# R's low channels as row tiles beside K, and the mix as two vector operations, in a convolution and channel-mix kernel

## Chip, cores, metric

The kernel runs on one core of one Trainium2 chip. The metric is the device time of one execution in microseconds (us), the median of several. The run-to-run spread of the kernel before is about 0.3%. Engines in what follows: PE is the tensor engine, PEld its weight loads, DVE the vector engine, ACT the scalar engine, POOL GpSimd, SP the engine that issues most of the stores and the transposing reads.

## The reference

x has 8 batches of 4160 tokens with 192 channels. A causal convolution over 7 tokens, with one softmaxed filter for each of 8 heads of 24 channels, gives y. Then comes a channel mix with 1024 hidden channels:

```python
x_prev = shift_by_one_token(y)
xk = mu_k * y + (1 - mu_k) * x_prev
xr = mu_r * y + (1 - mu_r) * x_prev
k = np.maximum(xk @ w_k, 0.0)            # 192 -> 1024
v = k * k @ w_v                          # 1024 -> 192
r = 1.0 / (1.0 + np.exp(-(xr @ w_r)))    # 192 -> 192
out = r * v
```

## The kernel before

Batches are worked in four pairs. The 192 channels are split in 128 high ones (rows 0 to 127 of a tile) and 64 low ones; the low channels of the pair's two batches share one tile, rows 0 to 63 and 64 to 127. A *step* is 512 tokens of both batches; it takes four *bundles* of two *slots*, each slot 128 hidden channels of K for 1024 columns. At each pair's end a *tail* step does the last 64 tokens.

The low part of K runs as two 64-row matmuls side by side (row tiles). R uses full-height matmuls for both parts; for its low part the weight rows that belong to the other batch are zero:

```python
def k_mm(n):                                   # one slot; cut
    for f in range(nf):
        for i in range(2):
            r = slice(0, P) if hi else slice(i * LO, (i + 1) * LO)
            nc.tensor.matmul(out=ps[:, i, f * L : (f + 1) * L],
                             lhsT=wk[r, 0 if hi else 1, fs], rhs=xk[r, i if hi else 2, :L], ...)

def r_mm(m):                                   # one tile of 128 tokens of one batch; cut
    hi, lo, wlo = xr[:, st, c : c + P], xr[:, 2, c : c + P], wr[:, 2 + st, :]
    nc.tensor.matmul(out=o, lhsT=hi, rhs=wr[:, 0, :], start=True, stop=False)
    nc.tensor.matmul(out=o, lhsT=lo, rhs=wlo, start=False, stop=True)
```

A mix is one vector operation on the difference of neighbouring tokens:

```python
nc.vector.scalar_tensor_tensor(out=o, in0=d[r0:r1, sl, :L], scalar=mu[r0:r1, i, part : part + 1],
                               in1=yT[r0:r1, sl, c0 : c0 + L], op0=ALU.mult, op1=ALU.add)
```

The convolution runs ahead of K on PE in *groups* of 112-token blocks, several *chunks* of heads a group. ACT copies each chunk out of PSUM; the group is written to DRAM and read back transposed by DMA (the first groups of the first pair are transposed on PE instead). The kernel uses 8 banks of PSUM, the memory that matmuls write to: K holds two tiles of two banks, V two of one bank, and convolution, transposes and R share two tiles of one bank (`psM`, `bufs=2`).

## Time and profile before

| | kernel before |
|---|---|
| time, median of 4 runs | 469.4 us |
| span of the profiled run | 467.2 us |
| PE / DVE / ACT busy | 95% / 84% / 80% |
| PE's share of the chain that ended last | 91% |

PE is the bound. The lines that carry this stand in the prediction. The chain is followed back from the last instruction; an engine with a large busy share that is missing from it costs nothing at present (of this chain ACT has 2% and DVE 1%). For the comparison later, here are the stretches from one tail step's K to the next: start to the first tail, three pairs (the third, left out, takes 109.24 us like the second), and the drain (columns: stretch, length, then busy time and count of PE, PEld, DVE, ACT, POOL, granted PE clock, DMA share, GB/s).

```profile
0.00:128.87 128.87, 117.58 (x972) 76.38 (x987) 101.84 (x168) 100.13 (x158) 28.57 (x43) 0.97 0.93 152
128.87:238.11 109.24, 107.05 (x942) 72.18 (x955) 95.52 (x149) 92.62 (x134) 9.84 (x12) 1.00 0.75 153
...
347.35:453.25 105.90, 103.72 (x925) 70.25 (x939) 92.60 (x144) 85.45 (x116) 2.85 (x4) 1.00 0.43 108
453.25:467.20 13.95, 9.80 (x124) 9.57 (x122) 4.90 (x9) 3.80 (x7) 0.00 (x0) 0.93 0.28 93
```

The last pair is 3.3 us shorter because half of the convolution is left to do: 16 matmuls instead of 32. The 16 that are missing have 480 columns; at about 0.2 us each, an estimate from the 0.18 us between starts at 432 columns, they make 3.2 us.

### The profile page before, as it was taken

The page shows a single profiled execution, that of the slowest core. Times are in us where ns is not written, and L with a number is a line of the kernel's source. Part 1 is how long each engine was busy: PE and PEld are TensorE (multiplying, and loading weights), DVE is VectorE, ACT ScalarE, POOL GpSimd, SP SyncE. Part 2 cuts the span into 40 slices and gives each one's busy share as a digit, 9 for nine tenths or more (in the row PEclk, how much of TensorE's full clock was granted, in tenths as well). Part 3 has the DMA queues.
Part 4 walks back from the last instruction along what each step waited for, and adds up shares of the span by engine and source line. Part 5 has one row for each costly group of instructions (what it writes and reads, how often), then busy time and mean ns, then how long its engine had stood idle before and what let it go on. Part 6 is the DMA issues. An engine that isn't in the chain of part 4 may idle for free.

```text
span 467.2 us, 9868 instructions
## 1 busy us (share of the span) xinstructions
PE 445.2 (95%) x3892; PEld 300.6 (64%) x3954; DVE 390.4 (84%) x616; ACT 374.6 (80%) x549; POOL 51.1 (11%) x71
## 2 busy tenths in 40 slices
PE   7788999999999999999999999999999999999996
PEld 3454766666776666666676666666676666666676
DVE  2778988797998879889798989978898987999873
ACT  2489888988879797888879788888978888777771
POOL 5812211000010041000002041000002000000000
PEclk9799999999999999999999999999999999999999
DMA  7996699972459599945367679937157753511222
GB/s 89 160 174 106 162 197 156 233 200 68 127 142 183 148 139 229 181 129 139 93 173 119 165 133 214 229 100 187 52 152 138 173 135 100 153 65 56 69 69 94
DMA packets 138942, 65.79 MB, mean 141 GB/s; under 512 B 89936, under 2 KB 138464, under 8 KB 138896
## 3 DMA queue, kind: packets, MB, share of 16 engines
q1 hardware_dynamic: 98000, 49.26, 41.0%
q0 software_dynamic: 40896, 15.90, 30.0%
q8 instruction: 31, 0.51, 0.4%
q14 instruction: 15, 0.12, 0.1%
HBM read 31.59 MB, written 37.52 MB: 148 GB/s over the span
## 4 chain that ended last, share of the span: by engine, by line
PE 91%; ACT 2%; issue 2%; DMA 2%; DVE 1%; DVEq 0%; ACTq 0%
PE ps_k L343 38%; PE ps_v L433 37%; PE ps_c L199 5%; PE ps_r L416 5%; PE ps_r L415 5%; ACT k_sb L372 1%; DMA w_scr<-w_row 1%; PE ps_k L360 1%; DMA toe<-w_scr 1%; ACT y L219 1%; DMA w_raw<-in_weight_dram 1%; PE ps_t L257 1%; DVE yT L268 0%; ACT y L222 0%; DVE k L391 0%
## 5 line engine op out<-in xcount | busy, mean ns | idle before, releaser
L372 ACT ACTIVATE k_sb<-ps_k 128x1024 bf16<-128x1024 f32 x260 | 260.2, 1026 | 35.8 <-PE ps_k L343 31.8
L343 PE MATMUL ps_k<-xk,wk 64*128 64x512 bf16 (+2 forms) x994 | 206.0, 376 | 9.5 <-ACT k_sb L372 0.9
L433 PE MATMUL ps_v<-wv,k 128*128 128x192 bf16 x2048 | 210.8, 246 | 0.0
L433 PEld LDWEIGHTS <-k 128*128 128x128 bf16 x2048 | 175.4, 98 | 30.6 <-issue 1.4
L391 DVE TENSOR_TENSOR k<-k_sb 128x1024 bf16<-128x1024 bf16 x256 | 174.8, 684 | 16.7 <-ACT k_sb L372 16.0
L343 PEld LDWEIGHTS <-wk 64*128 64x128 bf16 (+1 forms) x1056 | 56.2, 96 | 109.2 <-issue 107.9
L446 DVE TENSOR_TENSOR o_sb<-ps_v,r_sb 128x384 f32<-128x384 f32 x132 | 72.2, 547 | 39.6 <-PE ps_v L433 34.7
L423 ACT ACTIVATE r_sb<-ps_r 128x384 bf16<-128x384 f32 x132 | 64.3, 487 | 38.1 <-PE ps_r L416 37.3
L301 DVE SCALAR_TENSOR_TENSOR xr<-d,mu,yT 128x1024 bf16<-128x1024 bf16 (+1 forms) x66 | 65.1, 988 | 0.1
L301 DVE SCALAR_TENSOR_TENSOR xk<-d,mu,yT 128x1024 bf16<-128x1024 bf16 (+1 forms) x66 | 64.4, 977 | 0.2
L415 PE MATMUL ps_r<-wr,xr 128*128 128x192 bf16 x256 | 62.8, 246 | 0.0
L416 PE MATMUL ps_r<-wr,xr 128*128 128x192 bf16 x256 | 62.8, 246 | 0.0
L219 ACT CAST y<-ps_c 112x480 bf16<-112x480 f32 (+4 forms) x100 | 47.9, 483 | 10.4 <-PE ps_c L199 10.2
L199 PE MATMUL ps_c<-xb,toe 128*112 128x480 bf16 (+5 forms) x152 | 46.2, 332 | 5.3 <-DMA toe<-w_scr 2.9
L109 POOL DMA_DIRECT2D xb<-in_x_dram x38 | 34.9, 928 | 26.8 <-PE ps_c L199 15.9
L281 DVE TENSOR_TENSOR d<-yT 128x1536 bf16<-128x1536 bf16 (+2 forms) x37 | 31.8, 859 | 0.4 <-DMA yT<-y_dram 0.2
L108 POOL DMA_DIRECT2D xb<-in_x_dram x8 | 4.3, 538 | 215.7 <-PE ps_k L343 206.3
L199 PEld LDWEIGHTS <-toe 128*112 128x112 bf16 x152 | 19.2, 134 | 12.1 <-DMA toe<-w_scr 3.4
L222 ACT CAST y<-ps_c 112x480 bf16<-112x480 f32 (+8 forms) x53 | 25.2, 482 | 0.2 <-DVE yT L227 0.2
L415 PEld LDWEIGHTS <-xr 128*128 128x128 bf16 x256 | 25.0, 98 | 0.0
L416 PEld LDWEIGHTS <-xr 128*128 128x128 bf16 x256 | 25.0, 98 | 0.0
L103 POOL DMA_DIRECT2D xb<-in_x_dram x8 | 4.6, 581 | 62.4 <-PE ps_r L416 61.0
(46 smaller groups left out, 67.8 us busy)
## 6 DMA issues: line engine op xcount, KB each, us to landing
out_dram<-o_sb SPq DMA_DIRECT2D x128, 192.0 KB, 2.3
y_dram<-y SPq DMA_DIRECT2D x7, 840.0 KB, 5.0
xb<-in_x_dram POOLq DMA_DIRECT2D x12, 432.0 KB, 12.0
y_dram<-y SPq DMA_DIRECT2D x6, 756.0 KB, 4.6
xb<-in_x_dram POOLq DMA_DIRECT2D x8, 480.0 KB, 13.2
xb<-in_x_dram POOLq DMA_DIRECT2D x6, 384.0 KB, 6.6
y_dram<-y SPq DMA_DIRECT2D x2, 504.0 KB, 10.7
xb<-in_x_dram POOLq DMA_DIRECT2D x4, 240.0 KB, 5.3
```

The lines of the kernel that those rows point to most:

```text
L109: nc.gpsimd.dma_start(out=xb[:, lo:hi, s, :], in_=bass.AP(tensor=x.tensor, offset=x.offset + (b * S + t0 + lo * BLK) * D, ap=[[D, P], [BLK ...
L199: nc.tensor.matmul(out=ps[:BLK, :, :, i * G : (i + 1) * G], lhsT=toe[:, h, :], rhs=xbs[g][:, :nb, :, h * G : (h + 1) * G], start=True, sto ...
L219: copy(out=yh[:, :, :, c0 : c0 + n], in_=ps[:BLK, :, :, 0:n])
L301: nc.vector.scalar_tensor_tensor(out=o, in0=d[r0:r1, sl, :L], scalar=mu[r0:r1, i, part : part + 1], in1=yT[r0:r1, sl, c0 : c0 + L], op0=AL ...
L343: nc.tensor.matmul(out=ps[:, i, f * L : (f + 1) * L], lhsT=wk[r, 0 if hi else 1, fs], rhs=xk[r, i if hi else 2, :L], start=start and f == ...
L372: nc.scalar.activation(out=k_sb, in_=ps.rearrange("p a b -> p (a b)"), func=AF.Relu)
L391: nc.vector.tensor_tensor(out=o, in0=i, in1=i, op=ALU.mult)
L415: nc.tensor.matmul(out=o, lhsT=hi, rhs=wr[:, 0, :], start=True, stop=False)
L416: nc.tensor.matmul(out=o, lhsT=lo, rhs=wlo, start=False, stop=True)
L423: nc.scalar.activation(out=r_sb[:, :n, :], in_=ps[:, :n, :], func=AF.Sigmoid)
L433: nc.tensor.matmul(out=o, lhsT=k2[:, f, t * P : (t + 1) * P], rhs=wv[:, f, :], start=(f == 0), stop=(f == NF - 1),)
L446: nc.vector.tensor_tensor(out=o_sb[:, :n, :], in0=v_ps.pop(m)[:, :n, :], in1=r_sbs.pop(m)[:, :n, :], op=ALU.mult)
```

## The change

R's low channels are to use the row tiles that K has open anyway. A tile of V and R now covers 128 tokens of both batches, so that R's two low matmuls are a pair. The two matmuls of such a pair write to two banks, as K's do, so `psM` becomes one tile of two banks, which R and the convolution share. Each mix becomes a scaling and an addition in bf16. The whole schedule is rewritten by bundle. The diff, cut to its core:

```diff
-    WARM = 34
+    WARM = 46
-    psM = ctx.enter_context(tc.tile_pool(name="psM", bufs=2, space=bass.MemoryType.PSUM))
+    psM = ctx.enter_context(tc.tile_pool(name="psM", bufs=1, space=bass.MemoryType.PSUM))
 # groups of the first pair, (blocks, step, transposed on PE):
-  (3,0,T) (4,1,T) (5,2,T) (4,3,T) (10,4,F) (6,6,F) (6,7,F)
+  (3,0,T) (4,1,T) (5,2,T) (4,3,T) (5,4,T) (5,5,T) (5,6,F) (5,7,F) (2,8,F)
+    def m_banks():
+        shared[:] = [psM.tile([P, 2, BANK], FP32, tag="m", name="ps_m"), 2]
+        return shared[0]
+
+    def m_bank():                      # a convolution chunk takes one of the two banks
+        if shared[1] != 1:
+            m_banks()
+            shared[1] = 0
+        shared[1] += 1
+        return shared[0][:, shared[1] - 1, :]
-        ps = psM.tile([P, 3, 2, BLK], BF16, tag="m", name="ps_t")
+        ps = psV.tile([P, 3, 2, BLK], BF16, tag="v", name="ps_t")    # transposes
-            go(t[:, 0:2, :L], slice(0, 2), 0, P)      # one scalar_tensor_tensor
+            nc.vector.tensor_scalar(out=o, in0=d[:, sl, :L], scalar1=mu[:, i, part : part + 1], scalar2=None, op0=ALU.mult)
+            nc.vector.tensor_tensor(out=o, in0=o, in1=yT[:, sl, c0 : c0 + L], op=ALU.add)
+    def r_part(m, hi, start):
+        for i in range(2):
+            r = slice(0, P) if hi else slice(i * LO, (i + 1) * LO)
+            nc.tensor.matmul(out=r_ps[m][:, i, :D], lhsT=xr[r, i if hi else 2, cs],
+                             rhs=wr[r, 0 if hi else 1, :], start=start, stop=not start)
 # one bundle, in program order:
+  K0 high, K0 low, K1 low, R low, K1 high, R high, relu 0, sigmoid, relu 1, V,
+  square 0, difference and mixes, square 1, r*v, then for each chunk: convolution matmuls, its copies; transposes
 # how far ahead things are, in bundles of the step's (or group's) own start:
-  transposed read 8.5   difference 3.5   V from the second bundle after the step's last
+  transposed read 8     difference 5     V from the first bundle after the step's last
```

More of the change, by code (lines that the diff above doesn't have):

```diff
@@ L52 @@
     psV = ctx.enter_context(tc.tile_pool(name="psV", bufs=2, space=bass.MemoryType.PSUM))
-    psM = ctx.enter_context(tc.tile_pool(name="psM", bufs=2, space=bass.MemoryType.PSUM))
+    psM = ctx.enter_context(tc.tile_pool(name="psM", bufs=1, space=bass.MemoryType.PSUM))
     dram = ctx.enter_context(tc.tile_pool(name="dram", bufs=1, space=bass.MemoryType.DRAM))
     steps = []
-    slots = []
+    bundles = []
     first_step = {}
@@ L64 @@
         for L in sizes + [TAIL]:
-            ns = L * NF // STEP if L > TAIL else 1
-            steps.append((p, t0, L, len(slots), ns))
-            slots += [(len(steps) - 1, j) for j in range(ns)]
+            nb = L * NF // STEP // 2 if L > TAIL else 1
+            steps.append((p, t0, L, len(bundles), nb))
+            bundles += [(len(steps) - 1, j) for j in range(nb)]
             t0 += L
-    NSLOT = len(slots)
+    NBUN = len(bundles)
+    tiles = []
+    for s, (p, t0, L, b0, nb) in enumerate(steps):
+        for c in range(max(1, L // P)):
+            tiles.append((s, c, max(b0 + nb, tiles[-1][2] + 1) if tiles else b0 + nb))
     groups = []
@@ L75 @@
         for nb, s, on_pe in (
-            ((3, 0, True), (4, 1, True), (5, 2, True), (4, 3, True), (10, 4, False), (6, 6, False), (6, 7, False))
+            ((3, 0, True), (4, 1, True), (5, 2, True), (4, 3, True), (5, 4, True), (5, 5, True), (5, 6, False), (5, 7, False), (2, 8, False))
             if p == 0
@@ L135 @@
     wk = const.tile([P, 2, DF], BF16)
-    wr = const.tile([P, 4, D], BF16)
+    wr = const.tile([P, 2, D], BF16)
     wv = const.tile([P, NF, D], BF16)
@@ L147, in load_wr @@
         nc.gpsimd.dma_start(out=wr[:, 0, :], in_=moe_w_r[0:P, :])
-        for i in (1, 2):
-            nc.gpsimd.dma_start(out=wr[0:LO, i, :], in_=moe_w_r[P:D, :])
-        for i in (1, 3):
-            nc.gpsimd.dma_start(out=wr[LO:P, i, :], in_=moe_w_r[P:D, :])
+        nc.gpsimd.dma_start(out=wr[0:LO, 1, :], in_=moe_w_r[P:D, :])
+        nc.gpsimd.dma_start(out=wr[LO:P, 1, :], in_=moe_w_r[P:D, :])
     def load_wv():
@@ L184 @@
     ys, yTs, y_drams = {}, {}, {}
+    shared = [None, 0]
+    def m_banks():
[7 more added lines that the diff above has]
+        return shared[0][:, shared[1] - 1, :]
     conv_ps = {}
@@ L189, in chunks, with conv_mm @@
         return [range(h, min(H, h + n)) for h in range(0, H, n)]
-    def conv_mm(g, c, pool=None, tag="m"):
+    def conv_mm(g, c, pool=None):
         nb = groups[g][2]
@@ L195, in conv_mm @@
         hs = chunks(g)[c]
-        ps = (pool or psM).tile([P, nb, 2, G * len(hs)], FP32, tag=tag, name="ps_c")
+        ps = pool.tile([P, BANK], FP32, tag="v", name="ps_c") if pool else m_bank()
+        ps = ps[:, : nb * 2 * G * len(hs)].rearrange("p (n s c) -> p n s c", n=nb, s=2)
         conv_ps[g, c] = ps
@@ L277, in diff @@
         c0 = YC + t0
-        d = two.tile([P, 3, STEP], BF16, tag="diff", name="d")
+        d = three.tile([P, 3, STEP], BF16, tag="diff", name="d")
         diffs[s] = d
@@ L292, in mix @@
         d, yT = diffs[s], yTs[p]
-        if part == 0 and L > TAIL:
+        if L > TAIL and s not in (xks, xrs)[i]:
             if i == 0:
@@ L316, in mix @@
                 go(tl[LO:P, i, 0, TAIL : 2 * TAIL], 2, LO, P)
-        elif part == 0:
-            go(t[:, 0:2, :L], slice(0, 2), 0, P)
-        else:
-            go(t[:, 2, :L], 2, 0, P)
-    k_ps, k_sbs, k2s = {}, {}, {}
-    def k_mm(n):
-        s, j = slots[n]
-        p, _, L, _, _ = steps[s]
-        if L == TAIL:
-            return k_mm_tail(n, p)
+        else:
+            sl = slice(0, 2) if part == 0 else slice(2, 3)
+            o = t[:, sl, :L]
+            nc.vector.tensor_scalar(
+                out=o, in0=d[:, sl, :L], scalar1=mu[:, i, part : part + 1], scalar2=None, op0=ALU.mult
+            )
+            nc.vector.tensor_tensor(out=o, in0=o, in1=yT[:, sl, c0 : c0 + L], op=ALU.add)
@@ L331, in k_mm, with k_part @@
+    k_ps, k_sbs, k2s = {}, {}, {}
+    def k_part(b, u, hi, start):
+        s, j = bundles[b]
+        L = steps[s][2]
         xk = xks[s]
-        ps = psK.tile([P, 2, BANK], FP32, tag="k", name="ps_k")
-        k_ps[n] = ps
-        first = j % 2 == 0
+        if start:
+            k_ps[b, u] = psK.tile([P, 2, BANK], FP32, tag="k", name="ps_k")
+        ps = k_ps[b, u]
         nf = STEP // L
-        def go(hi, start):
-            for f in range(nf):
-                fs = slice((j * nf + f) * P, (j * nf + f + 1) * P)
-                for i in range(2):
-                    r = slice(0, P) if hi else slice(i * LO, (i + 1) * LO)
-                    nc.tensor.matmul(
-                        out=ps[:, i, f * L : (f + 1) * L],
-                        lhsT=wk[r, 0 if hi else 1, fs],
-                        rhs=xk[r, i if hi else 2, :L],
-                        start=start and f == 0,
-                        stop=not start and f == nf - 1,
-                    )
@@ L351, in k_mm @@
-        go(first, True)
-        go(not first, False)
-    def k_mm_tail(n, p):
+        for f in range(nf):
+            fs = slice(((2 * j + u) * nf + f) * P, ((2 * j + u) * nf + f + 1) * P)
+            for i in range(2):
+                r = slice(0, P) if hi else slice(i * LO, (i + 1) * LO)
+                nc.tensor.matmul(
+                    out=ps[:, i, f * L : (f + 1) * L],
+                    lhsT=wk[r, 0 if hi else 1, fs],
+                    rhs=xk[r, i if hi else 2, :L],
+                    start=start and f == 0,
+                    stop=not start and f == nf - 1,
+                )
@@ L355, in k_mm_tail, with k_tail @@
+    def k_tail(b):
+        p = steps[bundles[b][0]][0]
         ps = psK.tile([P, NF, 2 * TAIL], FP32, tag="k", name="ps_k")
-        k_ps[n] = ps
+        k_ps[b, 0] = ps
         for f in range(NF):
@@ L366, in k_mm_tail, with k_relu, k_square @@
                 )
-    def k_relu(n):
-        ps = k_ps.pop(n)
+    def k_relu(b, u):
+        ps = k_ps.pop((b, u))
         k_sb = four.tile([P, 2 * STEP], BF16, tag="k_sb", name="k_sb")
-        k_sbs[n] = k_sb
+        k_sbs[b, u] = k_sb
         nc.scalar.activation(out=k_sb, in_=ps.rearrange("p a b -> p (a b)"), func=AF.Relu)
-    def k_square(n):
-        s, j = slots[n]
+    def k_square(b, u):
+        s, j = bundles[b]
         L = steps[s][2]
-        k_sb = k_sbs.pop(n)
+        i = k_sbs.pop((b, u))
@@ L378, in k_square @@
         if L == TAIL:
             k2s[s] = two.tile([P, NF, 2 * TAIL], BF16, tag="k2t", name="k2t")
-            i = k_sb
             o = k2s[s].rearrange("p a b -> p (a b)")
         else:
-            if j == 0:
+            if j == 0 and u == 0:
                 k2s[s] = three.tile([P, NF, 2 * STEP], BF16, tag="k2", name="k2")
             nf = STEP // L
-            i = k_sb
-            o = k2s[s][:, j, :]
+            f0 = (2 * j + u) * nf
+            o = k2s[s][:, f0, :]
             if nf > 1:
-                i = k_sb.rearrange("p (b f t) -> p f b t", b=2, f=nf)
-                o = k2s[s][:, j * nf : (j + 1) * nf, 0 : 2 * L].rearrange("p f (b t) -> p f b t", b=2)
+                i = i.rearrange("p (b f t) -> p f b t", b=2, f=nf)
+                o = k2s[s][:, f0 : f0 + nf, 0 : 2 * L].rearrange("p f (b t) -> p f b t", b=2)
@@ L391, in k_square @@
         nc.vector.tensor_tensor(out=o, in0=i, in1=i, op=ALU.mult)
-    tiles = []
-    for s, (p, t0, L, n0, ns) in enumerate(steps):
-        for t in range(max(1, 2 * L // P)):
-            at_ = n0 + ns + 2
-            tiles.append((s, t, max(at_, tiles[-1][2] + 1) if tiles else at_))
-    r_ps, r_sbs, v_ps = {}, {}, {}
-    def r_mm(m):
-        s, t, _ = tiles[m]
-        p, _, L, _, _ = steps[s]
-        q = m - t % 2
-        if t % 2 == 0:
-            r_ps[q] = psM.tile([P, 2, D], FP32, tag="m", name="ps_r")
-        o = r_ps[q][:, t % 2, :]
-        if L > TAIL:
-            xr = xrs[s]
-            st, c = divmod(t * P, L)
-            hi, lo, wlo = xr[:, st, c : c + P], xr[:, 2, c : c + P], wr[:, 2 + st, :]
-        else:
-            hi, lo, wlo = tails[p % 2][:, 1, 1, :], tails[p % 2][:, 1, 0, :], wr[:, 1, :]
-        nc.tensor.matmul(out=o, lhsT=hi, rhs=wr[:, 0, :], start=True, stop=False)
-        nc.tensor.matmul(out=o, lhsT=lo, rhs=wlo, start=False, stop=True)
+    r_ps, r_sbs, v_ps = {}, {}, {}
@@ new lines, in r_part @@
+    def r_part(m, hi, start):
+        s, c, _ = tiles[m]
+        xr = xrs[s]
+        if start:
+            r_ps[m] = m_banks()
+        cs = slice(c * P, (c + 1) * P)
+        for i in range(2):
+            r = slice(0, P) if hi else slice(i * LO, (i + 1) * LO)
+            nc.tensor.matmul(
+                out=r_ps[m][:, i, :D],
+                lhsT=xr[r, i if hi else 2, cs],
+                rhs=wr[r, 0 if hi else 1, :],
+                start=start,
+                stop=not start,
+            )
@@ L418, in r_sig, with r_tail @@
+    def r_tail(m):
+        t = tails[steps[tiles[m][0]][0] % 2]
+        r_ps[m] = m_banks()
+        for i in range(2):
+            nc.tensor.matmul(
+                out=r_ps[m][:, 0, :D], lhsT=t[:, 1, 1 - i, :], rhs=wr[:, i, :], start=i == 0, stop=i == 1
+            )
     def r_sig(m):
-        ps = r_ps.pop(m)
-        n = 2 if steps[tiles[m][0]][2] > TAIL else 1
         r_sb = four.tile([P, 2, D], BF16, tag="r_sb", name="r_sb")
         r_sbs[m] = r_sb
-        nc.scalar.activation(out=r_sb[:, :n, :], in_=ps[:, :n, :], func=AF.Sigmoid)
+        n = 2 if steps[tiles[m][0]][2] > TAIL else 1
+        nc.scalar.activation(out=r_sb[:, :n, :], in_=r_ps.pop(m)[:, :n, :D], func=AF.Sigmoid)
@@ L425, in v_mm @@
     def v_mm(m):
-        s, t, _ = tiles[m]
-        q = m - t % 2
-        if t % 2 == 0:
-            v_ps[q] = psV.tile([P, 2, D], FP32, tag="v", name="ps_v")
-        o = v_ps[q][:, t % 2, :]
-        k2 = k2s[s]
-        for f in range(NF):
-            nc.tensor.matmul(
-                out=o,
-                lhsT=k2[:, f, t * P : (t + 1) * P],
-                rhs=wv[:, f, :],
-                start=(f == 0),
-                stop=(f == NF - 1),
-            )
+        s, c, _ = tiles[m]
@@ L441, in v_out @@
+        L = steps[s][2]
+        n = 2 if L > TAIL else 1
+        ps = psV.tile([P, 2, D], FP32, tag="v", name="ps_v")
+        v_ps[m] = ps
+        for i in range(n):
+            for f in range(NF):
+                nc.tensor.matmul(
+                    out=ps[:, i, :],
+                    lhsT=k2s[s][:, f, i * L + c * P : i * L + (c + 1) * P],
+                    rhs=wv[:, f, :],
+                    start=(f == 0),
+                    stop=(f == NF - 1),
+                )
     def v_out(m):
-        s, t, _ = tiles[m]
+        s, c, _ = tiles[m]
@@ L449, in v_out @@
         if L > TAIL:
-            st, c = divmod(t * P, L)
+            t = t0 + c * P
             nc.sync.dma_start(
-                out=out[2 * p + st, t0 + c : t0 + c + 2 * P, :].rearrange("(m p) d -> p m d", p=P),
-                in_=o_sb,
+                out=out[2 * p : 2 * p + 2, t : t + P, :].rearrange("b t d -> t b d"), in_=o_sb
             )
@@ L459, in v_out, with conv, tr, x_in @@
                 )
-    early, pe, act, dve = ({} for _ in range(4))
+    early, side, mid = ({} for _ in range(3))
     def at(table, n, fn, *a):
+        assert n >= 0, (fn, a)
         table.setdefault(n, []).append((fn, a))
-    for g, (p, blk0, nb, n0, on_pe) in enumerate(groups):
+    act_, dve_ = nc.scalar.copy, nc.vector.tensor_copy
+    def conv(g, c, copy):
+        conv_mm(g, c)
+        conv_out(g, c, copy)
+    def tr(g, j):
+        tr_mm(g, j)
+        tr_out(g, j, dve_)
+    def x_in(g):
+        x_tile(g, nc.vector)
+        load_x(g)
+    START = {2: (0, 2), 3: (2, 2), 4: (4, 2), 5: (6, 1), 6: (9, 1), 7: (13, 1), 8: (18, 1)}
+    for g, (p, blk0, nb, b0, on_pe) in enumerate(groups):
         if g < 2:
@@ L470 @@
         nc_ = len(chunks(g))
-        late = p == 0 and n0 < 30
-        if not on_pe:
-            per = 2 if late else 1
-            c0 = n0 - 20 if late else n0 - 30
-            w0, r0 = c0 + -(-nc_ // per), n0 - (11 if late else 17)
-        else:
-            per = 1
-            c0 = n0 - 14 if n0 > 12 else 1
-            r0 = c0 + nc_ + 1
+        if p == 0:
+            c0, per = START[g]
+        else:
+            c0, per = b0 - 18, 1
         if g > 3:
-            at(early, max(c0 - 14, 6 if g == 4 else 10), x_tile, g, nc.vector)
-            at(early, max(c0 - 14, 6 if g == 4 else 10), load_x, g)
+            at(early, max(c0 - 4, 0), x_in, g)
         for c in range(nc_):
-            at(pe, c0 + c // per, conv_mm, g, c)
-            at(act, c0 + c // per + 1, conv_out, g, c, nc.scalar.copy)
+            at(side, c0 + c // per, conv, g, c, act_)
+        e = c0 + -(-nc_ // per)
         if on_pe:
             for j in range((nb + 1) // 2):
-                at(pe, r0 + j, tr_mm, g, j)
-                at(dve, r0 + 1 + j, tr_out, g, j, nc.vector.tensor_copy)
-        else:
-            at(dve, w0, y_write, g)
-            at(dve, r0, y_read, g)
-    for s, (p, t0, L, n0, ns) in enumerate(steps):
+                at(side, e + j // 3, tr, g, j)
+        else:
+            at(side, e - 1, y_write, g)
+            at(side, e + 2, y_read, g)
+    for s, (p, t0, L, b0, nb) in enumerate(steps):
         if s == 0:
             continue
-        late = n0 < 14
-        at(dve, n0 - (3 if late else 7), diff, s)
-        for j, (i, part) in enumerate(((0, 0), (0, 1), (1, 0), (1, 1))):
-            at(dve, n0 + ((-3, -2, -1, 0)[j] if late else j - 5), mix, s, i, part)
-    for m, (s, t, vs) in enumerate(tiles):
-        at(pe, vs - 2, r_mm, m)
-        if t % 2 == 1 or steps[s][2] == TAIL:
-            q = m - t % 2
-            at(act, vs - 1, r_sig, q)
-            at(dve, vs + 1, v_out, q)
-        at(pe, vs, v_mm, m)
+        late = 3 if b0 == 2 else 2 if b0 == 6 else 0
+        at(mid, max(0, b0 - 5 + late), diff, s)
+        at(mid, max(0, b0 - 4 + late), mix, s, 0, 0)
+        at(mid, max(0, b0 - 3 + late) if b0 > 2 else 1, mix, s, 0, 1)
+        at(mid, b0 - 2 + (late > 0), mix, s, 1, 1)
+        at(mid, b0 - 1 + (late > 0), mix, s, 1, 0)
+    tile_of = {b: m for m, (_, _, b) in enumerate(tiles)}
     def run(table, n):
@@ L523, in prologue @@
         nc.vector.memset(w_row, 0.0)
-        nc.vector.memset(wr[:, 2:4, :], 0.0)
         load_x(0)
@@ L552, in prologue @@
             nc.gpsimd.memset(t, 0.0)
-        dve_, act_ = nc.vector.tensor_copy, nc.scalar.copy
         n = len(chunks(0))
         for c in range(n):
-            conv_mm(0, c, psV if c % 2 else None, "v" if c % 2 else "m")
+            conv_mm(0, c, psV if c % 2 else None)
         for c in range(n):
@@ L564, in prologue @@
         for c in range(n):
-            conv_mm(1, c, psV if c % 2 else None, "v" if c % 2 else "m")
+            conv_mm(1, c, psV if c % 2 else None)
             conv_out(1, c, act_)
@@ L575, in prologue @@
         load_x(3)
-    def bundles():
-        n = 0
-        while n < tiles[-1][2] + 3:
-            w = 2 if n < NSLOT and steps[slots[n][0]][2] > TAIL else 1
-            yield range(n, n + w)
-            n += w
     with tc.manual_schedule():
         prologue()
-        for n in range(-60, 0):
-            for table in (early, act, pe, dve):
-                assert n not in table, n
-        for ns in bundles():
-            for n in ns:
-                run(early, n)
-            real = [n for n in ns if n < NSLOT]
-            for n in real:
-                k_mm(n)
-            for n in ns:
-                run(act, n)
-                run(pe, n)
-                if n in real:
-                    k_relu(n)
-                run(dve, n)
-                if 1 <= n <= NSLOT:
-                    k_square(n - 1)
+        for b in range(tiles[-1][2] + 2):
+            run(early, b)
+            m = tile_of.get(b)
+            r_in_full = m is not None and steps[tiles[m][0]][2] == TAIL
+            slots = 0
+            if b < NBUN:
+                slots = 1 if steps[bundles[b][0]][2] == TAIL else 2
+            if slots == 2:
+                k_part(b, 0, True, True)
+                k_part(b, 0, False, False)
+                k_part(b, 1, False, True)
+            elif slots:
+                k_tail(b)
+            if m is not None and not r_in_full:
+                r_part(m, False, True)
+            if slots == 2:
+                k_part(b, 1, True, False)
+            if r_in_full:
+                r_tail(m)
+            elif m is not None:
+                r_part(m, True, False)
+            if slots:
+                k_relu(b, 0)
+            if m is not None:
+                r_sig(m)
+            if slots == 2:
+                k_relu(b, 1)
+            if m is not None:
+                v_mm(m)
+            if slots:
+                k_square(b, 0)
+            run(mid, b)
+            if slots == 2:
+                k_square(b, 1)
+            if m is not None:
+                v_out(m)
+            run(side, b)
 _INS = ['x', 'weight', 'moe_mu_k', 'moe_mu_r', 'moe_w_k', 'moe_w_v', 'moe_w_r']
```

## The prediction

> **What bounds the kernel now.** I read the page's busy shares and chain first, to find the engine that sets the end, then long windows, then the timeline of single bundles, and the groups by form for the price of each instruction. A bundle is two slots of K matmuls (1024 output columns each) with the V and R tiles between them.
>
> ```profile
> PE 445.2 (95%) x3892; PEld 300.6 (64%) x3954; DVE 390.4 (84%) x616; ACT 374.6 (80%) x549; POOL 51.1 (11%) x71
> PE ps_k L343 38%; PE ps_v L433 37%; PE ps_c L199 5%; PE ps_r L416 5%; PE ps_r L415 5%; ACT k_sb L372 1%; DMA w_scr<-w_row 1%; PE ps_k L360 1%; DMA toe<-w_scr 1%; ACT y L219 1%; DMA w_raw<-in_weight_dram 1%; PE ps_t L257 1%; DVE yT L268 0%;
> ```
>
> The chain that ended last is matmuls: K 38%, V 37%, R 10%, convolution 5%. DVE's 84% and ACT's 80% do not appear in it. The windows say where the tensor engine is short of work (columns: length, busy time and count of PE, PEld, DVE, ACT, POOL, then granted clock, DMA share, GB/s).
>
> ```profile
> 16.00:20.00 4.00, 3.45 (x24) 2.62 (x23) 3.93 (x9) 1.68 (x5) 3.85 (x7) 0.50 1.45 159
> 20.00:24.00 4.00, 3.88 (x35) 2.31 (x34) 3.93 (x6) 3.08 (x4) 2.15 (x3) 0.82 1.25 133
> ...
> 238.27:347.51 109.24, 107.06 (x942) 72.18 (x955) 95.53 (x149) 92.62 (x134) 9.86 (x12) 1.00 0.75 153
> ```
>
> The last row is the third pair of batches, from one tail step to the next: 98% busy at full clock. The first two are the start, at a granted clock of 0.50 and 0.82. One whole bundle on the tensor engine looks like this (start, length, operation, count; the two rows of 64*128 are from narrower windows of the same timeline, and one K matmul is missing from the trace):
>
> ```profile
> 280.35 0.25 PE L415 MATMUL ps_r<-wr,xr 128*128 128x192 bf16 x1
> 280.43 0.25 PE L416 MATMUL ps_r<-wr,xr 128*128 128x192 bf16 x1
> 280.51 1.67 PE L343 MATMUL ps_k<-xk,wk 128*128 128x512 bf16 x7
> ...
> 281.04 0.39 PE L343 MATMUL ps_k<-xk,wk 64*128 64x512 bf16 x2
> 281.27 0.38 PE L343 MATMUL ps_k<-xk,wk 64*128 64x512 bf16 x2
> ...
> 282.02 0.35 PE L199 MATMUL ps_c<-xb,toe 128*112 128x432 bf16 x1
> 282.20 0.82 PE L433 MATMUL ps_v<-wv,k 128*128 128x192 bf16 x8
> ...
> 284.03 0.38 PE L343 MATMUL ps_k<-xk,wk 128*128 128x512 bf16 x1
> ```
>
> Only starts count: a matmul is shown 0.25 us long but the next starts 0.08 us later, so busy time overstates its cost threefold. The starts give: R and V 0.0825 us per 192 columns, a convolution of 432 columns 0.18, the K block 1.51 (280.51 to 282.02). K is four full passes of 512 columns and two pairs of 64-row matmuls; six passes of 0.216 us are 1.295, so the two changes between full rows and row tiles cost about 0.21 together. A bundle without convolution is 1.51 + 4 x 0.0825 (R) + 16 x 0.0825 (V) = 3.16 us. With these prices a pair is 32 x 3.16 + 1.7 (tail) + 6.1 (convolution) = 108.9, against 109.24 in the window: in the steady state nothing but issued matmul columns makes the time. Over the whole run I get about 428 us of issue between the first K at 19.3 and the last tail step at 453.2 us, 434 us long: about 6 us of stalls, nearly all before 50 us.
>
> [...]the two 64-row halves start together (281.04), the next pair 0.23 us later, and each change costs about 0.1 us. [...]a square of 1024 takes 684 ns; the one-operation mix takes 1279 ns for the same 1024[...]. No tensor_scalar of this size is in it.[...]
>
> **The change, part by part.**
>
> ```profile
> L415 PE MATMUL ps_r<-wr,xr 128*128 128x192 bf16 x256 | 62.8, 246 | 0.0
> L416 PE MATMUL ps_r<-wr,xr 128*128 128x192 bf16 x256 | 62.8, 246 | 0.0
> L301 DVE SCALAR_TENSOR_TENSOR xk<-d,mu,yT 128x1024 bf16<-128x1024 bf16 x31 | 39.6, 1279 | 0.2
> ...
> L301 DVE SCALAR_TENSOR_TENSOR xr<-d,mu,yT 128x512 bf16<-128x512 bf16 x33 | 24.6, 745 | 0.0
> ```
>
> R's low channels (L416): 256 full-height matmuls against zero-padded weights become 128 pairs of 64-row matmuls that run together, inside the stretch where K is in row tiles already, so no change of mode is added. A pair should cost one pass, 0.0825 us, plus about 0.01 of pair overhead (0.23 against 0.216 above). Saved: 256 x 0.0825 - 128 x 0.093 = 21.1 - 11.9 = **9.2 us**, all on the path. Three bundles at the very end have V and R but no K; there the mode changes are new: 3 x 0.2 = +0.6.
>
> The mix: scaling and addition in place of one operation. [...]off the path: worth **0** where PE sets the pace.
>
> The first pair: two more groups (ten blocks) go through PE transposes rather than DMA: 30 x 0.05 to 0.08 = about 2 us of PE. Smaller convolution groups add about 0.5. Part of this falls into the stalls of the start; I count **+2**. Twelve more warm-up matmuls (12 x 0.216 = 2.6 us from 10.3) end at about 12.9, just before the convolution's weights land at 13.2; the first K (2.48 us cold, 1.51 warm) and the first convolutions could save 1.0 to 1.5, but ACT and DVE chains follow at once; I count **-1**.
>
> Sum: -9.2 + 0.6 + 2 - 1 = -7.6. For new waits in the steady state and the first pair I add +0.5, for an earlier first V (a bundle sooner) -1. 469.6 - 8.1 = **461.5 us**, 1.7% faster.
>
> **The rivals.** *A wait replaces the work removed (lag and PSUM).* V of a step now follows its last K bundle by one bundle, not two, and the squares wait behind a mix and a difference in one bundle of four. With prices above I find the last square 2.0 us into the next bundle, its matmul at 2.35: 0.3 us to spare. R and convolution share one PSUM buffer: the convolution's copy (ACT, 0.56 us) ends about 4.1 us after its bundle's start, R's low pair of the next wants the banks at 4.27. Both are close; if both miss by 0.1 us on every bundle, 128 x 0.1 = 13 us goes and the time is 470 to 474. Against it: the estimates leave a margin, and ACT and DVE have 15 to 20% to spare.
>
> *A transfer becomes exposed.* The transposed read now precedes the difference that needs it by three bundles (10 us) rather than five.
>
> ```profile
> yT<-y_dram SPq DMA_TRANSPOSE x15, 6.0
> ```
>
> The median is 6.0 us, the slowest 13.5 and 10.8; each slow one could hold DVE 2 to 4 us, and the two-bundle lead in the first pair is tighter still. That makes 464 to 467.
>
> *The start shrinks more.* If full clock and the earlier V take away half of the 6 us of stalls, and the added transposes all fall into what is left, the time is 457 to 459.
>
> **Range and chances.** The 9.2 us is the firm part; the start and the two close waits are each worth a few us either way. Predicted 461.5, range 457 to 468. The 2% line is at 460.2, only 1.3 us below the middle, so faster by over 2%: 0.36; within 2%: 0.60; slower needs both waits to miss badly: 0.04.
>
> **What would show it.** Right: a bundle without convolution of about 3.08 us, between tail steps about 106.8 us instead of 109.24; the R low pair 0.09 us after the K pair before it; [...]PE still 95% of the chain. Wrong: PE idle that the profile puts to ACT copies of the convolution (PSUM) or to the squares, a DVE that waits for the transposed read, [...]or a R low pair that costs two passes, in which case hardly anything is gained.

What is cut above are statements that no trace or run of this case shows, and figures worked out from them: among them the forecast time of a scaling, what DVE was to save by it, and the DVE busy time expected from it. ("In it", said of a tensor_scalar, is the trace of the kernel before.) The sum: -9.2 + 0.6 + 2 - 1 = -7.6, then +0.5 and -1, so -8.1 and 461.5 us; the mix counts 0 in it. The 0.3 us to spare for the last square may count a mix at a price that is cut. The -1 for twelve more warm-up matmuls is the author's estimate from one place in the trace of before: the granted clock is 1.00 up to 13.2 us, PE idles 2.86 us before the first convolution, and the clock is then 0.75 from 13.2 to 16 us and 0.50 from 16 to 20; the first K takes 2.48 us there (19.26 to 21.74) against 1.51 later. That a filled gap keeps the clock up was not shown then; with 46 warm-up matmuls the changed kernel shows 1.00 from 12 to 24 us and a first K of 1.52 us (18.85 to 20.37).

## The result, and the profile after

| | before | after |
|---|---|---|
| time, median of 4 runs | 469.4 us | 490.9 us |
| range of the runs | 469.0 to 470.7 | 486.2 to 491.0 |
| span of the profiled run | 467.2 us | 489.3 us |
| ratio of fast runs, 95% interval | | 1.0429 [1.0364, 1.0493] |

The change made the kernel 4.3% slower. A ratio here is the mean time of one kernel's fast runs over that of the other's from the same rounds, so it is not quite the ratio of the medians. One of the four was 4.6 us faster than the others (486.2 us); its trace was not kept, so why is open.

The page of the changed kernel: busy shares, and the chain.

```profile
PE 456.3 (93%) x4012; PEld 298.2 (61%) x4012; DVE 390.8 (80%) x753; ACT 384.1 (78%) x546; POOL 53.2 (11%) x73
...
PE 76%; DMA 11%; DVE 6%; ACT 5%; issue 2%; ACTq 0%; DVEq 0%
```

PE's share of the chain fell from 91% to 76%, and DMA took 11%. So the question is not whether R became cheaper but what PE waits for. The steady bundle first, from PE's timeline (start, length, operation, count):

```profile
281.25 1.13 PE L361 MATMUL ps_k<-xk,wk 128*128 128x512 bf16 x6
282.22 0.25 PE L418 MATMUL ps_m<-wr,xr 64*128 64x192 bf16 x2
282.40 0.60 PE L361 MATMUL ps_k<-xk,wk 128*128 128x512 bf16 x2
282.84 0.33 PE L418 MATMUL ps_m<-wr,xr 128*128 128x192 bf16 x2
283.00 1.48 PE L448 MATMUL ps_v<-wv,k 128*128 128x192 bf16 x16
284.32 0.35 PE L218 MATMUL ps_m<-xb,toe 128*112 128x432 bf16 x1
284.51 0.38 PE L361 MATMUL ps_k<-xk,wk 128*128 128x512 bf16 x1
```

From K to K is 284.51 - 281.25 = 3.26 us with one convolution of 432 columns (0.18 us), so 3.08 us without, the figure that the prediction named. The saving in R is there. The stretches from tail to tail say where it is lost:

```profile
0.00:144.62 144.62, 125.49 (x1061) 80.94 (x1062) 104.31 (x213) 103.93 (x156) 30.23 (x45) 0.98 0.73 118
144.62:259.07 114.45, 109.75 (x956) 71.42 (x955) 95.34 (x182) 95.30 (x135) 10.09 (x12) 0.97 0.77 147
259.07:372.12 113.05, 108.56 (x955) 70.43 (x954) 95.06 (x180) 95.28 (x135) 10.10 (x12) 0.98 0.73 148
372.12:475.79 103.67, 103.48 (x938) 67.58 (x937) 91.63 (x172) 86.05 (x117) 2.82 (x4) 1.00 0.49 118
475.79:489.30 13.51, 9.00 (x108) 7.83 (x106) 4.44 (x8) 3.49 (x7) 0.00 (x0) 0.95 0.25 82
```

Against before: first pair +15.8, second +5.2, third +3.8, last -2.2, drain -0.4, together the 22 us. The last pair has half the convolution and no bundle with two chunks, and none of its differences waits for a transposed read (its three land in 6.1 to 7.1 us). It is faster by just the predicted saving, 9.2 / 4 = 2.3 us. The list of waits names what stands behind the others (who waited, for whom, us in total, times, longest):

```profile
DVE d L300 <- DMA yT<-y_dram: 9.4, 2, 4.8
PE ps_v L448 <- DVE k L406: 9.4, 5, 4.5
...
PE ps_m L218 <- ACT y L241: 6.7, 8, 1.6
...
PE ps_m L218 <- ACT y L238: 4.6, 4, 1.6
PE ps_t L276 <- DVE o_sb L461: 4.4, 3, 2.5
```

Three causes can be read here. **One:** the convolution waits twelve times, 11.3 us, for ACT's copy of a convolution. All twelve lie in bundles with two chunks, where the second chunk waits for the copy of the first. **Two:** the difference waits twice for the transposed read, and V behind it. **Three:** transposes, now in V's PSUM tiles, wait for V's results to be taken out, 4.4 us. The first two are the main suspects. The timeline of the second cause:

```profile
205.37 9.49 SPq L261 DMA_TRANSPOSE yT<-y_dram  x1
...
214.07 0.74 PE L448 MATMUL ps_v<-wv,k 128*128 128x192 bf16 x7
...
217.70 0.96 DVE L300 TENSOR_TENSOR d<-yT 128x1536 bf16<-128x1536 bf16 x1 [4.82 <-DMA yT<-y_dram]
218.58 0.69 DVE L406 TENSOR_TENSOR k<-k_sb 128x1024 bf16<-128x1024 bf16 x1
...
219.32 1.62 PE L448 MATMUL ps_v<-wv,k 128*128 128x192 bf16 x9 [4.51 <-DVE k L406]
```

The read is issued at 205.4 and lands 12.3 us later. The difference waits for it; the square stands behind the difference in DVE's queue; V has done seven of its matmuls and waits at the eighth for that square. PE is idle for 4.5 us, and the stall does not end there:

```profile
214.80:219.30 4.50, 0.01 (x1) 0.00 (x0) 1.60 (x3) 0.88 (x1) 0.00 (x0) 0.90 0.89 171
219.30:223.00 3.70, 3.68 (x18) 1.94 (x18) 3.19 (x6) 0.84 (x3) 0.00 (x0) 0.50 0.16 53
```

After it the granted clock is 0.50 for the next 3.7 us (last columns: clock, DMA share, GB/s). This is part of why the second pair is 5.2 us longer although R saves it more than 2. The kernel before has the same slow read (landing 10.8 us after issue at 184.3), but its difference comes at 199.0, 3.9 us after the landing. In both kernels the read is issued when its group's write to DRAM has landed (before, written at 175.0 and landed 9.2 us later, read at 184.3; after, 194.65, 10.7 and 205.4), so the lead counts from the write: before, 24.0 us from the write's issue (175.0) to the difference for 20.0 us of write and read; after, 18.2 us (194.65 to 212.9, when DVE is free for the difference) for 23.0 us. So the transfers were slow in both, 3.0 us slower after, and the change gave away 5.8 us of the lead that hid them.

### The profile page after: what moved, and what is told of

It reads as the page before. It is cut to its first block, busy times and chain, and to the rows that moved or that the text cites. A ratio compares the mean times of both kernels' runs of the same rounds, so it can differ in the third digit from the quotient of the medians.

```text
span 489.3 us, 10124 instructions
## 1 busy us (share of the span) xinstructions
PE 456.3 (93%) x4012; PEld 298.2 (61%) x4012; DVE 390.8 (80%) x753; ACT 384.1 (78%) x546; POOL 53.2 (11%) x73
## 4 chain that ended last, share of the span: by engine, by line
PE 76%; DMA 11%; DVE 6%; ACT 5%; issue 2%; ACTq 0%; DVEq 0%
PE ps_k L361 33%; PE ps_v L448 29%; DMA y_dram<-y 6%; PE ps_m L418 6%; DMA yT<-y_dram 5%; PE ps_m L218 5%; ACT k_sb L388 3%; PE warm L557 3%; DVE k L406 2%; ACT y L238 1%; DVE d L300 1%; PE ps_k L376 1%; PE ps_t L276 1%; ACT y L241 1%; DVE o_sb L461 0%
## 5 line engine op out<-in xcount | busy, mean ns | idle before, releaser
L361 PE MATMUL ps_k<-xk,wk 64*128 64x512 bf16 (+2 forms) x1056 | 226.4, 381 | 0.2
L448 PEld LDWEIGHTS <-k 128*128 128x128 bf16 x2048 | 172.2, 98 | 11.2 <-DVE k L406 10.8
L238 ACT CAST y<-ps_m 112x480 bf16<-112x480 f32 (+8 forms) x95 | 46.9, 494 | 42.8 <-PE ps_m L218 34.4
L418 PE MATMUL ps_m<-wr,xr 64*128 64x192 bf16 (+1 forms) x512 | 74.3, 248 | 0.0
L438 ACT ACTIVATE r_sb<-ps_m 128x384 bf16<-128x384 f32 x132 | 64.0, 485 | 7.5 <-PE ps_m L418 6.2
L418 PEld LDWEIGHTS <-xr 64*128 64x128 bf16 (+1 forms) x512 | 41.3, 97 | 45.9 <-issue 3.9
L218 PE MATMUL ps_m<-xb,toe 128*112 128x432 bf16 (+5 forms) x161 | 45.6, 318 | 11.3 <-ACT y L241 6.7
L342 DVE TENSOR_TENSOR xk<-xk,yT 128x1024 bf16<-128x1024 bf16 (+1 forms) x66 | 36.2, 549 | 2.3
L342 DVE TENSOR_TENSOR xr<-xr,yT 128x512 bf16<-128x512 bf16 (+1 forms) x66 | 36.3, 549 | 2.3
L241 ACT CAST y<-ps_m 112x480 bf16<-112x480 f32 (+8 forms) x52 | 24.3, 467 | 6.0 <-PE ps_m L218 3.6
L339 DVE TENSOR_SCALAR xr<-d,mu 128x512 bf16<-128x512 bf16 (+1 forms) x66 | 27.5, 416 | 0.0
L339 DVE TENSOR_SCALAR xk<-d,mu 128x1024 bf16<-128x1024 bf16 (+1 forms) x66 | 27.1, 410 | 0.2
```

Of the source, the lines that this page charges most:

```text
L218: nc.tensor.matmul(out=ps[:BLK, :, :, i * G : (i + 1) * G], lhsT=toe[:, h, :], rhs=xbs[g][:, :nb, :, h * G : (h + 1) * G], start=True, sto ...
L238: copy(out=yh[:, :, :, c0 : c0 + n], in_=ps[:BLK, :, :, 0:n])
L339: nc.vector.tensor_scalar(out=o, in0=d[:, sl, :L], scalar1=mu[:, i, part : part + 1], scalar2=None, op0=ALU.mult)
L342: nc.vector.tensor_tensor(out=o, in0=o, in1=yT[:, sl, c0 : c0 + L], op=ALU.add)
L361: nc.tensor.matmul(out=ps[:, i, f * L : (f + 1) * L], lhsT=wk[r, 0 if hi else 1, fs], rhs=xk[r, i if hi else 2, :L], start=start and f == ...
L418: nc.tensor.matmul(out=r_ps[m][:, i, :D], lhsT=xr[r, i if hi else 2, cs], rhs=wr[r, 0 if hi else 1, :], start=start, stop=not start,)
```

## The experiments

Nine further kernels ran, all with correct results. Times are medians of four fast runs unless said otherwise; the kernel before was 468.9 to 469.2 us in the same rounds.

### Convolution matmuls of a bundle before the copies (e1_mm_first)

```diff
-            at(side, c0 + c // per, conv, g, c, act_)        # matmuls, then copies
+            at(side_mm, c0 + c // per, conv_mm, g, c)        # run first, for all chunks of the bundle
+            at(side, c0 + c // per, conv_out, g, c, act_)
```

> Changed kernel, with both convolution matmul groups of a bundle issued before either copy. In the trace of the changed kernel, the second group of the twelve bundles that hold two waits 0.6 to 1.75 us for the ACT copy of the first, 13.3 us in sum, though the two lie in different banks of one tile. Theory PSUM (the wait comes from program order within the shared two-bank tile: copy first, then the second write): those waits go and the time falls by 8 to 13 us from 491, to 478 to 483. Rival ACT (ACT is the bound of the start, so PE waits for it somewhere in any order): under 3 us, the idle time moves to K or R matmuls.

Measured: 483.3 us, ratio 1.0318 [1.0269, 1.0367]. The twelve waits are gone, but the gain, 7.6 us by the medians, is just under the range that I gave. The list of waits shows one reason: K now waits for a mix of the first step (3.6 us in 2 waits), and DVE still waits 8.0 us for the transposed read. Some of the idle time only moved. (The waits were 11.3 us by the list, 0.4 to 1.6 us each, not the 13.3 of my expectation.) Not all of the gain is the edit's either: of the 9.0 us between the profiled runs, 5.6 lie in the first pair, where the twelve waits were, and 3.9 in the third, which has no such wait; there the stall of the difference on the read fell from 4.6 to 2.3 us, because that read landed 9.0 us after its issue instead of 11.5. The pure ACT rival (under 3 us) is out all the same.

### Differences and mixes later (e2_diff_later)

```diff
-        late = 3 if b0 == 2 else 2 if b0 == 6 else 0
+        late = 3 if b0 == 2 else 2
```

> Changed kernel, with the differences and mixes of nearly all steps two bundles later (differences three bundles ahead of their K instead of five). Theory lead (the transposed read of a pair's last group lands late and holds DVE, and the squares and V behind it, 4.7 and 4.5 us): both stalls go, and the 0.36 us waits of V for a square behind a difference too; 480 to 483 us. Rival transfers (the transfers themselves became slow and something else, the next K, waits for them): 488 to 491.

Measured: 482.4 us, ratio 1.0305 [1.0273, 1.0337]. The second and third pair fell from 114.45 and 113.05 to 108.27 and 108.04 us:

```profile
146.38:254.65 108.27, 106.77 (x956) 70.36 (x954) 95.66 (x182) 95.35 (x135) 9.79 (x12) 1.00 0.81 157
```

No difference waits for a transposed read any more, although the slowest read between 180 and 235 us still takes 11.8 us to land (12.3 in the changed kernel). So the lead was the cause: with it restored, a read about as slow costs nothing. New small waits came: K waits for mixes that now come just in time, 3.3 us in 6 waits.

### Both (e3_both)

> Changed kernel with both edits, matmul groups before copies and differences later. If the two causes are separate, the gains add: 491 - 11 - 9 = 471, from 467 to 474. If one hides the other, 476 or more. What then remains over my prediction of 461.5 is the transposes' wait for the V buffers (4.9 us in the trace) and the rest of the start.

Measured: 470.9 us, ratio 1.0057 [1.0026, 1.0088]. The gains more than add: 7.6 and 8.5 us alone, 20.0 together. In the profiled runs the order of the matmuls makes the first pair 5.6 us shorter alone and 11.9 us after the later differences (146.38 to 134.43). The waits for copies that it takes away were 13.8 us there, not 11.3, and one of them was 4.1 us long; the rest of the interaction is open. So the two causes are both real but not independent, and the 471 of my expectation, which took 11 and 9 us, was met partly by luck. Both edits bring the changed kernel to within 0.6% of the kernel before, but not below it.

### R's low channels at full height again, on top of both (e4_both_full_r)

The loads of the padded weights and their zero fill, not shown in the cut below, come back too.

```diff
-                r_part(m, False, True)       # low, as row tiles, between K1 low and K1 high
-                r_part(m, True, False)       # high
+                r_part(m, True, True)        # high
+                r_part(m, False, False)      # low at full height, zero-padded weights wr[:, 2 + i, :]
```

> The kernel with both edits, and R's low channels back at full height with zero-padded weights after the high ones, as in the kernel before. Theory PE (steady state is nothing but matmul columns): it is slower than the kernel with both edits by 128 x (2 x 0.0825 - 0.093) = 9.2 us, range 7.5 to 10.5. Rival (another engine or a wait sets the bundle): under 3 us.

Measured: 484.2 us, 13.3 more than with both edits, above the range. The steady bundle in PE's timeline gives the cause of the larger part:

```profile
281.36 1.67 PE L363 MATMUL ps_k<-xk,wk 128*128 128x512 bf16 x8
282.86 0.49 PE L419 MATMUL ps_m<-wr,xr 128*128 128x192 bf16 x4
283.19 1.48 PE L449 MATMUL ps_v<-wv,k 128*128 128x192 bf16 x16
284.51 0.35 PE L220 MATMUL ps_m<-xb,toe 128*112 128x432 bf16 x1
284.69 0.38 PE L363 MATMUL ps_k<-xk,wk 128*128 128x512 bf16 x1
```

It is 3.33 us against 3.26. From tail to tail the pairs take 110.67, 110.54 and 107.11 us against 108.27, 108.04 and 104.62 with both edits: 2.4 to 2.5 us a pair, so about 9.8 us for four (an estimate from three), close to the predicted 9.2. The remaining 3.6 us lie before the first tail. The first K waits 0.4 us there for a load of R's weights. R waits 3.3 us for a convolution copy at 93 us, against 1.1 with both edits: ACT's copy itself waits for an earlier group's write of y to land, 4.2 us against 1.4, before it can fill that y buffer again (there are two). These waits are not R's matmul time.

### The mix as one operation again, on top of both (e5_both_stt)

```diff
-            nc.vector.tensor_scalar(out=o, in0=d[:, sl, :L], scalar1=mu[:, i, part : part + 1], ...)
-            nc.vector.tensor_tensor(out=o, in0=o, in1=yT[:, sl, c0 : c0 + L], op=ALU.add)
+            go(o, sl, 0, P)                  # scalar_tensor_tensor
```

> The kernel with both edits (matmul groups first, differences later: 470.9 us) with each mix back as one scalar-tensor-tensor operation. Scaling and addition of 1024 take 481 and 695 ns in the trace of the changed kernel and cannot overlap[...]. Theory (the mix is off the path and no faster on DVE): within 1.5 us of 470.9. Rival (two operations are what makes K and V wait for DVE): 2 us or more faster; rival two (they do help DVE): 2 us or more slower.

Measured: 473.6 us, ratio to the kernel before 1.0087 [1.0067, 1.0107], against 1.0057 [1.0026, 1.0088] with the two-operation mix. That is 2.7 us by the medians, beyond my 1.5, but the intervals overlap. The pairs after the first take 108.15, 107.99 and 104.57 us, within 0.12 us of the two-operation version, so the steady state does not feel the mix at all. By the starts of 1024-element mixes scaling and addition take 1.12 us (0.51 and 0.61) in the trace of the changed kernel, the single operation 1.20 in that of before; of 512, 0.77 against 0.66. With two of each a step the one nearly makes up for the other. What differs, 3.1 us between the profiled runs, lies before the first tail. The largest part is again R's wait behind a copy that waits for a write of y: 2.8 us against 1.1. The run with two tiles, below, keeps the two-operation mix and has it too, 2.6 us. So at least this wait is not the mix's own; the rest is not settled.

### The kernel before with the two-operation mix alone (e7_before_two_op_mix)

The same edit the other way round, on the kernel before.

> The kernel before with nothing changed but the mixes of the full steps as a scaling and an addition. Theory (off the path): the same time as before, within 1 us. If DVE had been a hidden bound, 2 us or more away in either direction.

Measured: 469.5 us, ratio 1.0015 [0.9998, 1.0032]: the same. DVE is busy 388.9 us instead of 390.4. This half of the change neither helps nor harms here, where PE is the bound.

### Two tiles of one bank instead of one of two (e9_two_tiles)

The second edit (later differences) is kept; the order is again matmuls, copies, matmuls, copies.

```diff
-        shared[:] = [psM.tile([P, 2, BANK], FP32, tag="m", name="ps_m"), 2]
+        return [psM.tile([P, BANK], FP32, tag=f"m{i}", name="ps_m") for i in range(2)]
...
-        if shared[1] != 1: ...               # a bank of the shared tile
+        shared[1] = 1 - shared[1]
+        return psM.tile([P, BANK], FP32, tag=f"m{shared[1]}", name="ps_m")
```

> The run with later differences alone (482.4 us), order of matmuls and copies as in the changed kernel, but the shared two-bank tile split in two tiles of one bank each; R's sigmoid becomes two operations on one bank each, which adds about 0.2 us of ACT a bundle. Theory (the program's waits go by whole tile in PSUM, though the banks differ): the twelve waits of the second group for the first's copy go without any change of order; start and first pair as in the run with both edits (tail step at about 134 us instead of 146), 471 to 476 in all as ACT has room. Rival (the hardware or the ACT queue makes the second group wait, and only order helps): the waits stay, 482 or more.

(The 0.2 us is an estimate: in the trace of the changed kernel a sigmoid of 384 elements takes 490 ns and one of 192 326 ns, so two of 192 would take 0.16 us more.)

Measured: 472.5 us, ratio 1.0065 [1.0031, 1.0099], against 482.4 with later differences alone. No convolution group waits for a copy any more, with the order unchanged. Some of the time moved here too: the first tail comes at 137.6 us, not 134.4, and by the list of waits K waits 2.3 us once for a copy. With the shared tile, PE's timeline of the changed kernel in the first bundle has

```profile
20.37 0.37 PE L218 MATMUL ps_m<-xb,toe 128*112 128x240 bf16 x2
22.25 0.36 PE L218 MATMUL ps_m<-xb,toe 128*112 128x240 bf16 x2 [1.51 <-ACT y L238]
```

and with two tiles the four matmuls are one row:

```profile
20.00 0.57 PE L214 MATMUL ps_m<-xb,toe 128*112 128x240 bf16 x4
```

So neither the hardware nor ACT's queue made the second chunk wait. The program's own semaphores did: with both banks in one PSUM tile and the copy first in program order, the write to the second bank waited for the reader of the first, in the changed kernel twelve times, 0.4 to 1.6 us each; with two tiles, or with the write first (e1_mm_first), not once.

### A tuned version (e6_tuned), and its warm-up (e8_tuned_warm34)

On top of the matmul order, four further waits were taken away. The edits, cut:

```diff
+        # difference 3 bundles ahead, both K mixes 2 ahead, R mixes 1 and 0 ahead;
+        # for step 1 the first three stand before the squares of bundle 0
-                at(side, e + j // 3, tr, g, j)
+                at(side, e + (j // 3 if g == 2 else j), tr, g, j)       # transposes spread over bundles
-            ys[g] = two.tile([P, GB, 2 * D], ...)
+            ys[g] = three.tile([P, GB, 2 * D], ...)
```

> Changed kernel with the matmul groups first and four further waits of the run with both edits taken away: mixes for K two bundles ahead of it together (waits of K for a mix: 6.8 us in 8 waits), step 1's difference and mix ahead of the first squares (2.4 us and a cold clock after it), transposes of groups 3 to 5 spread over bundles (2.6 us), a third y buffer (1.3 us). Theory (the steady state is as predicted and only schedule waits keep the time up): 457 to 463 us, 1.5 to 2.5% under the kernel before. Rival (these waits hide others): 467 or more.

Measured: 463.9 us, ratio 0.9888 [0.9873, 0.9902]: 1.1% faster than the kernel before, the best of all that ran, and 0.9 us over my range. Four edits went in together, so the run does not say what each was worth. (The cold clock of the expectation: in the run with both edits K waits 2.3 us at 25.2 us, and the six K matmuls after it take 1.54 us and V 2.27, against 1.14 and 1.48 in the next bundle.) Its stretches:

```profile
0.00:130.35 130.35, 122.63 (x1061) 79.12 (x1062) 101.22 (x205) 101.90 (x156) 30.18 (x45) 1.00 0.79 131
130.35:236.99 106.64, 106.64 (x956) 70.29 (x955) 95.09 (x183) 95.30 (x135) 9.83 (x12) 1.00 0.81 157
```

The second pair takes 106.64 us and the third 107.42, against 109.24 before and 106.8 predicted. The first takes 130.35, still 1.5 us more than the 128.87 of before although R saves it some 2.4 us; there the extra transposes, smaller convolution groups and what is left of the start's waits remain. I did not separate these.

> The same tuned kernel with 34 warm-up matmuls as in the kernel before. My predicted worth of the twelve more was 1 us: then it is 0.5 to 1.5 us slower than the tuned kernel, with a granted clock of 0.5 to 0.8 from 16 to 24 us. Rival (the start is held by ACT and DVE chains, and the warm-up itself delays the convolution by up to 0.7 us): same or faster.

Measured: 464.1 us, ratio 0.9895 [0.9880, 0.9909], against 0.9888 with 46. The clock is 0.50 from 16 to 24 us with 34 matmuls (expected 0.5 to 0.8) and 1.00 with 46, but the times cannot be told apart. (The first convolution starts at 13.19 us in the kernel before with 34, at 13.95 in the changed kernel and 13.43 with both edits, which have 46.) The profiled runs differ by 1.1 us, all of it before the first tail, but the one with 34 was the slowest of its four. That the chain of ACT and DVE work at the start absorbs the clock is a guess that no run tested.

## Why the prediction was wrong

**What held.** The bound and the price of a matmul by starts; the R low pair at one pass and the bundle of 3.08 us; the saving, 9.2 us predicted and 9.8 measured by its undoing; the mix off the path, shown on the kernel before; the steady-state time of a pair, 106.8 predicted, 106.6 and 107.4 in the tuned version. R's wait for the convolution's copy in PSUM, which I called close, did not bind in the steady bundles that the timelines show.

**The step that failed** is one term of the sum: "For new waits in the steady state and the first pair I add +0.5". It measured about 30 us, the 22 us by which the profiled span grew plus the 8 us that I expected to gain. The first two of these parts account for 20.0 us together, the third for 7.0; what then remains, 2.4 us over the prediction, was not separated:

1. *Two chunks in one bundle.* I priced the shared PSUM buffer only between a bundle's copy and the next bundle's R. I never asked about two chunks in the same bundle, as if two banks of one tile were independent. They wait in twelve bundles, 11.3 us by the list of waits; removing this gave 7.6 us alone (5.6 in the pair where the waits were) and 11.5 us after the other edit.
2. *The transposed read.* My second rival named this mechanism rightly, with the lead cut from five bundles to three, but priced a slow read at "2 to 4 us" of DVE and the whole at 464 to 467. Two reads held DVE 4.7 us each on average. The stall passed nearly whole to PE (4.5 and 4.3 us) because the square stood behind the difference, and after the first one the clock fell to 0.50. Removing it gave 8.5 us. I had seen the 10.8 us read and its landing, and should have subtracted: issue of the write and landing of the read against the time at which the new schedule wants it.
3. *The start.* Transposes in V's tiles wait 4.4 us, which no run tested alone. The tuned version took 7.0 us out of the run with both edits: 4.1 us before the first tail and the rest in the pairs, where mixes that came late with the second edit held K.

Two small terms were also off. The saving that I expected on DVE did not come: the scaling takes 481 ns for 1024 elements, and DVE saved nothing to speak of (busy 390.8 us after, 390.4 before). The twelve warm-up matmuls, counted at -1, have no effect that the times show. The +2 for the added transposes was not measured by itself.

One reading in the prediction was loose, without effect on the sum. ACT and DVE are not missing from the chain of the kernel before: they have 2% and 1% of it.

The prediction's closing list did name PE idle put to ACT copies and a DVE that waits for the transposed read as what would make it wrong. Both came. The weakness was that neither got a number from the new schedule, and that "the 9.2 us is the firm part" drew the middle of the range towards the part I could price.

## What to carry to other kernels

When a rewrite saves work on the bound and also moves the schedule, check each transfer, and the one that it waits for, against the new lead with its slowest landing in the trace, not its median, and check what stands behind its consumer in the same queue. Give things that should be independent in PSUM their own tiles, or issue all writes before the first read of the shared one: here either took away all twelve waits (by the lists 11.3 us in the changed kernel, 13.8 with later differences). Replacing one off-path vector operation by two was worth nothing here, where PE sets the pace: 469.5 us against 469.2.
